# Five tiles in the sweeps over the weight units, sign rows made in one go at the start, attention's operands loaded ahead of the weights, and a new search of the order

## The chip, the cores and the metric

The kernel runs on one core of one Trainium2 chip. A core has five engines, each with its own instruction queue worked off strictly in order: TensorE (PE, matrix products), VectorE (DVE), ScalarE (ACT), GpSimd (POOL) and SyncE (SP, which here issues every DMA). They wait for each other through semaphores. The metric is the device time of one execution in microseconds (us), lower is better; several executions are timed and the median is given.

## The reference

Two parts follow each other. The first is a chunked linear attention with decay (4 batches, 8 heads, 768 positions, head size 32, state size 16); the second multiplies its output with two weight matrices, with `h - tanh(h)` between them.

```python
cum = np.cumsum(la, axis=-1)                      # la = log(clip(a))
L = np.exp(cum[:, :, :, None] - cum[:, :, None, :]) * causal
M = np.einsum('bhin,bhjn->bhij', Cc, Bc) * L
y = np.einsum('bhij,bhjd->bhid', M, xc) + np.einsum('bhin,bhnd->bhid', Cc, state) * decay_to_i
state = decay_full * state + np.sum(Bx, axis=2)
...
x = attn_out.transpose(0, 2, 1, 3).reshape(3072, 256)
h = x @ w_in                                      # 3072 x 256 by 256 x 2048
out = (h - np.tanh(h)) @ w_out                    # 3072 x 2048 by 2048 x 256
```

`w_in` and `w_out` arrive as 64-bit floats, and the kernel makes 32-bit pairs of them itself.

## The kernel before, in words

**Second part.** The 3072 rows are 12 tiles of 256. The 2048 inner columns are 8 *units* of 256. One step (t, u) takes tile t through unit u: `mm1` (L646, twelve matmuls into `ph`), tanh on ACT (L661), the difference on DVE (L665), a rounded copy `gh` on ACT (L669) and the rest `gl` on DVE (L676), and `mm2` (L709, twelve matmuls into `o`). Each 32-bit operand is a rounded part plus a rest (`wh`, `wl`; `xh`, `xl`; `gh`, `gl`), and three of the four products are taken. Two steps named in `FULL`, (0, 0) and (0, 1), come before those parts are ready: they use the whole 32-bit operands (L630, L701). `conv(u)` turns unit u's raw 64-bit weights into `wh` and `wl`: two ACT passes (L348, L369) and five DVE passes (L353, L358, L361, L365, L372). `NSW` says how many tiles go through the weights in *sweeps* while those are still being converted: the first `NSW` tiles go through units 0 and 1, then all of them through 2 and 3, and so on (`SWEEPS`), with partial sums kept in `pt` tiles (L724, L731). The other tiles run through all eight units in one go.

**First part.** A batch's 768 positions are 7 chunks of up to 112, so there are 28 chunks. Chunks 0 to 2 belong to tile 0, 3 and 4 to tile 1, 5 and 6 to tile 2, and so on. For a chunk, PE makes the score products and the differences of `cum` into `att` (L512, L521), ACT takes the exponential (L536), DVE multiplies (L540), POOL clears the upper half (L543), and PE makes the output and the next state in `y` (L569, L575). ACT then copies the state into the next chunk's operand (four copies, L580) and the output into `xh` (L593), and DVE makes `xl` (L598); the next chunk's `y` needs those state copies. From chunk `joint` on, the products of the next chunk are issued together with this chunk's `y`. The three chunks of tile 0 use an older path (`first_tile`): PE makes `cp` from the logs `la` (L447, four matmuls for a half chunk), ACT takes the exponential with the bias `ncum` (L465), and DVE multiplies with `att` (L458 on PE, L470 on DVE). From chunk 3 on, the differences come from one matmul over 9 rows of `lt_c` and `rt_c`. Those rows are parts of `cum` (DVE makes `parts`, L875 to L879; a DMA puts them in DRAM, L882; eight DMAs for each of two spans of chunks bring them back, L888 and L890) beside rows of ones (`lt_c`, POOL memset, L827) and rows of signs (`rt_c`, L496: `lt_c`'s ones times a per-partition 0 or -1 `par`; four instructions, two for chunks 3 to 9 and two for chunks 10 to 27).

**The start.** `a` is loaded, clipped on DVE (L804) and its log taken on ACT (L840, `la`). PE makes the running sums `pr` and `pq` (L863, L868). Meanwhile PE runs `warm`, matmuls of ones that nothing reads (L834).

**What sets the order.** Every operation is registered with an engine and an assumed cost. A list scheduler walks through them with a priority per operation from the table `RANK`, and each engine's program is issued in the order of the starts that come out. Where the plan leaves PE idle for more than `SPARE` within its first 65 us, `fill` puts matmuls of ones there (L434), so many pieces as the gap holds, with `LATE` more for gaps over 2 us. They stand in PE's queue like any other instruction, and PE has to work them off before it goes on.

Of the kernel before, what the change touches and what calls it, by code (L numbers as in the profile page):

```python
# [15 lines left out]
ALU = mybir.AluOpType  # L16
# [26 lines left out]
NPH, NL, NSW, NRAW, NGB, LAG, WARM = 2, 3, 4, 2, 3, 2, 8  # L43
SWEEPS = 0, 2, 4, 6, 8
AHEAD = 32
LULL, SPARE, PIECE, LATE = 65.0, 0.35, 0.215, 1.4
NPT = 6
# [955 lines left out]
```

## Time and profile before

| | us |
|---|---|
| median of 3 runs | 336.06 |
| lowest and highest of them | 334.4, 338.8 |
| profiled execution: its own time | 337.54 |
| its span from first to last instruction | 335.8 |

Of the profile, busy shares of the engines say how much of the span an engine had an instruction running. A matmul of ones counts as busy too, and so does a matmul at half clock. So for PE the list of instructions in order of time has to be read beside the shares: it shows what is work and what is filler. In these lists a row begins with the start and the duration in us; the number behind "x" counts instructions, and the bracket at its end gives the idle time ahead and what ended it. A 32-bit matmul appears as two records, so a row of the program's order with x3 is x6 in the trace.

### The profile page before, as it was taken

How to read it: one execution, taken by the hardware profiler on the slowest of the kernel's cores; microseconds unless marked ns; L12 is line 12 of the kernel's file. 1: busy time of each engine (PE TensorE's matmuls, PEld its weight loads, DVE VectorE, ACT ScalarE, POOL GpSimd, SP SyncE). 2: the span in 40 equal slices, each digit the busy share in tenths (PEclk: the TensorE clock that was granted, in tenths of full speed). 3: DMA queues.
4: the chain of work that ended last, by engine and by line, in shares of the span. 5: the costliest groups of instructions: out<-in, count | busy, mean ns of one | idle time of the engine just before them, and what ended most of it. 6: DMA issues, size and time to landing. Idle time of an engine off the chain costs nothing.

```text
span 335.8 us, 9087 instructions
## 1 busy us (share of the span) xinstructions
PE 326.6 (97%) x3872; PEld 314.4 (94%) x3872; DVE 226.6 (67%) x332; ACT 192.0 (57%) x404; POOL 56.8 (17%) x74
## 2 busy tenths in 40 slices
PE   8899999999999999999999999999999999999995
PEld 6788789999999999999999999999999999999995
DVE  2779999999998975645555655655655655654552
ACT  5766888784775644344555645643656645644441
POOL 6543464610102110000011101101111101100000
PEclk9699999999999999999999999999999999999999
DMA  6939668640102102010011200200200100100000
GB/s 158 263 112 307 153 230 193 194 143 0 48 9 68 32 0 65 31 33 2 31 48 31 64 12 20 64 20 13 62 4 2 33 2 2 33 0 2 31 2 32
DMA packets 12472, 21.41 MB, mean 64 GB/s; under 512 B 2848, under 2 KB 7648, under 8 KB 12432
## 3 DMA queue, kind: packets, MB, share of 16 engines
q1 hardware_dynamic: 12432, 20.84, 21.9%
q8 instruction: 30, 0.49, 0.6%
q14 instruction: 10, 0.08, 0.1%
HBM read 17.51 MB, written 3.32 MB: 62 GB/s over the span
## 4 chain that ended last, share of the span: by engine, by line
PE 87%; DMA 4%; DVE 4%; issue 2%; ACT 1%; POOL 1%; SPq 1%; POOLq 0%
PE o L709 39%; PE ph L646 38%; PE y L569 4%; PE att L521 3%; DMA bc<-bc_d 3%; DMA raw<-w_d 2%; PE att L512 1%; PE cp L447 1%; PE y L575 1%; POOL lt L543 1%; DVE lt L470 1%; DVE wm L353 0%; DVE g L665 0%; PE att L458 0%; DVE rt_c L496 0%
## 5 line engine op out<-in xcount | busy, mean ns | idle before, releaser
L665 DVE TENSOR_TENSOR g<-ph,g 128x512 f32<-128x512 f32 x96 | 66.1, 690 | 55.9 <-ACT g L661 55.9
L661 ACT ACTIVATE g<-ph 128x512 f32<-128x512 f32 x96 | 57.5, 599 | 74.3 <-PE ph L646 71.7
L646 PE MATMUL ph<-xh,wh 128*128 128x256 f32 x376 | 95.3, 278 | 0.2 <-DVE g L665 0.2
L646 PE MATMUL ph<-xh,wl 128*128 128x256 f32 x376 | 94.5, 276 | 0.0
L676 DVE TENSOR_TENSOR gl<-g,gh 128x512 fp32r<-128x512 f32 x94 | 66.7, 713 | 26.6 <-ACT gh L669 24.0
L669 ACT CAST gh<-g 128x512 fp32r<-128x512 f32 x94 | 58.2, 619 | 36.0 <-DVE g L665 29.7
L646 PE MATMUL ph<-xl,wh 128*128 128x256 f32 x376 | 73.2, 276 | 0.0
L646 PEld LDWEIGHTS ph<-xh,wh 128*128 128x128 f32 x376 | 70.6, 188 | 0.8 <-DVE g L665 0.4
L646 PEld LDWEIGHTS ph<-xh,wl 128*128 128x128 f32 x376 | 70.6, 188 | 0.0
L709 PE MATMUL o<-gh,wh 128*128 128x256 f32 x376 | 60.2, 282 | 0.0
L709 PE MATMUL o<-gh,wl 128*128 128x256 f32 x376 | 57.9, 276 | 0.0
L709 PE MATMUL o<-gl,wh 128*128 128x256 f32 x376 | 57.9, 276 | 0.0
L646 PEld LDWEIGHTS ph<-xl,wh 128*128 128x128 f32 x376 | 56.6, 188 | 0.0
L709 PEld LDWEIGHTS o<-gh,wh 128*128 128x128 f32 x376 | 49.8, 188 | 1.1
L709 PEld LDWEIGHTS o<-gh,wl 128*128 128x128 f32 x376 | 49.6, 188 | 0.0
L709 PEld LDWEIGHTS o<-gl,wh 128*128 128x128 f32 x376 | 49.6, 188 | 0.0
L543 POOL TENSOR_SCALAR_AFFINE_SELECT lt<-lt 128x896 f32<-128x896 f32 (+1 forms) x25 | 28.6, 1143 | 122.3 <-DVE lt L540 109.5
L540 DVE TENSOR_TENSOR lt<-att,lt 128x896 f32<-128x896 f32 (+1 forms) x25 | 26.6, 1065 | 2.8 <-ACT lt L536 2.1
L396 POOL TENSOR_TENSOR bw<-braw,wdec 128x256 f32<-128x256 f32 x14 | 12.3, 886 | 90.7 <-PE y L575 89.9
L536 ACT ACTIVATE lt<-att 128x896 f32<-128x896 f32 (+1 forms) x25 | 22.6, 904 | 1.4 <-PE att L521 0.3
L580 ACT COPY x<-y 16x64 f32<-16x64 f32 x96 | 19.4, 202 | 6.4 <-DVE xl L598 3.5
L569 PE MATMUL y<-lt,x 128*32 128x112 f32 (+1 forms) x448 | 16.8, 268 | 1.9 <-POOL lt L543 1.2
(79 smaller groups left out, 264.1 us busy)
## 6 DMA issues: line engine op xcount, KB each, us to landing
raw<-w_d SPq DMA_DIRECT2D x16, 512.0 KB
x<-x_d SPq DMA_DIRECT2D x14, 256.0 KB
bc<-bc_d SPq DMA_DIRECT2D x56, 60.0 KB
out_d<-ob SPq DMA_DIRECT2D x16, 128.0 KB
braw<-bn_d SPq DMA_DIRECT2D x14, 112.0 KB
out_d<-pt SPq DMA_DIRECT2D x8, 128.0 KB
cum<-parts SPq DMA_DIRECT2D x1, 168.0 KB
lt_c<-cum SPq DMA_DIRECT2D x4, 27.0 KB
```

What stands on the lines that cost most here:

```text
L396: nc.gpsimd.tensor_tensor(out=d["b"].rearrange("p c (h n) -> p c h n", h=H), in0=d["braw"].rearrange("p c (h n) -> p c h n", h=H), in1=wd. ...
L536: nc.scalar.activation(k["l"][:, :, 0:q].rearrange("p (i w) q -> p i w q", i=4), place[1][:, :, 0:2, N : N + q], AF.Exp)
L540: nc.vector.tensor_tensor(out=lt, in0=place[1][:, :, 2:4, N : N + q], in1=lt, op=ALU.mult)
L543: nc.gpsimd.affine_select(out=k["l"][:, :, 0:q], in_=k["l"][:, :, 0:q], pattern=[[0, H], [1, q]], compare_op=ALU.is_ge, fill=0.0, base=N, ...
L569: nc.tensor.matmul(out=y[D * h : D * h + D, hg * Q : hg * Q + q], lhsT=d["x"][:, cg, P * hg + D * h : P * hg + D * h + D], rhs=k["l"][:, 4 ...
L580: nc.scalar.copy(grp[(ck + 1) // CPG]["x"][0:N, (ck + 1) % CPG, 2 * D * i : 2 * D * i + 2 * D], k["y"][D * i : D * i + N, H * D : H * D + ...
L646: nc.tensor.matmul(out=ph[:, j, :], lhsT=w_[:, u, 0, k, j * P : (j + 1) * P], rhs=d[("xh", "xl")[p]][:, k, ts], start=p == 0 and k == 0 an ...
L661: nc.scalar.activation(g, gs[t, u][0], AF.Tanh)
L665: nc.vector.tensor_tensor(out=g, in0=ph, in1=g, op=ALU.subtract)
L669: nc.scalar.copy(gh, gs[t, u][1])
L676: on.tensor_tensor(out=gl, in0=g, in1=gh.bitcast(F32), op=ALU.subtract)
L709: nc.tensor.matmul(out=po[t, seg][:, e, :], lhsT=w_[:, u, 1, j, e * P : (e + 1) * P], rhs=g[:, j, :], start=u == seg[0] and k == 0 and j = ...
```

## The change

- `NSW` goes from 4 to 5: tiles 0 to 4 go through the weights in sweeps. `joint` moves with it from chunk 10 to chunk 12, and three more sums into `pt` and one more copy take the place of the fifth tile's last copies. `NPT`, the number of `pt` buffers, goes from 6 to 7, and a smaller reserve (`dynamic_dma_scratch_size`) makes room for it.
- The four instructions that make the sign rows (L496, each behind `lt_c`'s ones) go. In their place DVE sets all of `rt_c` from chunk 3 on to 1 at the start, and multiplies it twice with `par`, the second time in place.
- `warm` grows from 8 to 10 matmuls.
- `LATE` shrinks from 1.4 to 0.6, and the planner's assumed lag behind a DMA grows, most for POOL.
- `RANK` is a new table, so nearly every instruction of the first 70 us stands elsewhere.

```diff
-NPH, NL, NSW, NRAW, NGB, LAG, WARM = 2, 3, 4, 2, 3, 2, 8
+NPH, NL, NSW, NRAW, NGB, LAG, WARM = 2, 3, 5, 2, 3, 2, 10
-LULL, SPARE, PIECE, LATE = 65.0, 0.35, 0.215, 1.4
-NPT = 6
+LULL, SPARE, PIECE, LATE = 65.0, 0.35, 0.215, 0.6
+NPT = 7
 RANK = """
-147 351 639 203 244 86 296 353 131 427 266 928 811 84 242 227 476 72 88 71 191 74 773 287 117 117 324 209 273 250 172
+21 1082 131 136 347 155 106 120 1250 704 221 751 237 279 665 53 610 117 277 109 215 33 80 335 59 1220 245 342 212 803
...
     def lag(self, a, b):
-        return self.DMA_LATENCY if a == "DMA" else 0.0 if a == b else self.SEM_PE if "PE" in (a, b) else self.SEM
+        if a == "DMA":
+            return {"POOL": 2.4, "DVE": 1.3, "ACT": 1.3}.get(b, self.DMA_LATENCY)
+        return 0.0 if a == b else self.SEM_PE if "PE" in (a, b) else self.SEM
...
-                for w in range(2):
-                    op("DVE", (0.45, 0.8)[s], lambda w=w, sl=sl: nc.vector.tensor_scalar(
-                           out=rt_c[:, w, sl], in0=lt_c[:, sl], scalar1=par[:, w : w + 1], scalar2=None, op0=ALU.mult),
-                       r=[l_c[s], "par", k["n_l"][1]], w=[r_c[s]])
...
+    sign = [rt_c[:, w, SPAN[0].start :].rearrange("p c m -> p (c m)") for w in range(2)]
+    op("DVE", 0.9, lambda: nc.vector.memset(sign[0], 1.0), w=r_c)
+    for w in (1, 0):
+        op("DVE", 0.95, lambda w=w: nc.vector.tensor_scalar(out=sign[w], in0=sign[0], scalar1=par[:, w : w + 1], scalar2=None,
+                                                            op0=ALU.mult), r=["par"], w=r_c)
...
-    nc = bacc.Bacc("TRN2", target_bir_lowering=False, num_devices=1)
+    nc = bacc.Bacc("TRN2", target_bir_lowering=False, num_devices=1, dynamic_dma_scratch_size=1024)
```

Three places of the new order matter below. The first is DVE's queue at its very start. Before, the clip of `a` (L804) stands right behind two small memsets:

```order
L790 MEMSET a_sb 32x32
L804 TENSOR_SCALAR a_sb<-a_sb 128x224
L807 TENSOR_SCALAR pid<-pid 128x1
L808 TENSOR_SCALAR pid<-pid 128x1
L809 CAST pidf<-pid 128x2
L810 CAST ncf<-ncol 128x16
L811 TENSOR_SCALAR par<-pidf 128x1
L812 TENSOR_SCALAR par<-pidf 128x1
L813 TENSOR_SCALAR idn<-ncf,pidf 128x16
L353 TENSOR_SCALAR wm_163<-raw_126 128x512
```

Now the same place of DVE's queue reads as follows (`rt_c` are the sign rows, 3200 numbers of two bytes on each partition):

```order
L790 MEMSET a_sb 32x32
L847 MEMSET rt_c 128x3200
L807 TENSOR_SCALAR pid<-pid 128x1
L808 TENSOR_SCALAR pid<-pid 128x1
L809 CAST pidf<-pid 128x2
L810 CAST ncf<-ncol 128x16
L811 TENSOR_SCALAR par<-pidf 128x1
L812 TENSOR_SCALAR par<-pidf 128x1
L813 TENSOR_SCALAR idn<-ncf,pidf 128x16
L849 TENSOR_SCALAR rt_c<-rt_c,par 128x3200 x2
L804 TENSOR_SCALAR a_sb<-a_sb 128x224
L882 CAST parts<-rows 112x2x128
```

The clip of `a`, from which the logs and all of attention follow, moved behind the constants and the three new instructions.

The second place is PE's queue from chunk 0's `y` to chunk 2's `y`. Before, with `pq` as the target of the filler:

```order
L569 MATMUL y_268<-lt_186,x_141 32x112 x8
L575 MATMUL y_268<-x_141,bw_212 16x32 x8
L458 MATMUL att<-bc_161 128x112 x8
L447 MATMUL cp_1_302<-upto,la 128x112 x4
L434 MATMUL pq_178<-const-float32-1.0 32x128 x3
L569 MATMUL y_331<-lt_234,x_141 32x112 x8
L575 MATMUL y_331<-x_141,bw_212 16x32 x8
L434 MATMUL pq_178<-const-float32-1.0 32x128 x22
L569 MATMUL y_403<-lt_287,x_144 32x112 x8
```

And now:

```order
L569 MATMUL y_266<-lt_196,x_133 32x112 x8
L575 MATMUL y_266<-x_133,bw_181 16x32 x8
L462 MATMUL att<-bc_156 128x112 x8
L451 MATMUL cp_1_305<-upto,la 128x112 x4
L438 MATMUL pq_165<-const-float32-1.0 32x128 x2
L569 MATMUL y_333<-lt_237,x_133 32x112 x8
L575 MATMUL y_333<-x_133,bw_181 16x32 x8
L438 MATMUL pq_165<-const-float32-1.0 32x128 x17
L569 MATMUL y_400<-lt_286,x_291 32x112 x8
```

The work is the same; six pieces of filler fewer stand in it. Behind it, three groups of filler of 5, 2 and 2 pieces become one of 11, which stands between chunk 6's `y` and the products of chunk 8.

The third place is SP's queue of DMAs at the start. Before:

```order
L315 DMA braw_99<-bn_d 112x256
L792 DMA a_sb<-a_d 112x192
L794 DMA a_sb<-a_d 96x32
L325 DMA raw_126<-w_d 128x1024
L294 DMA bc_128<-bc_d 16x960 x4
L325 DMA raw_126<-w_d 128x1024
L306 DMA x_141<-x_d 128x512
L306 DMA x_144<-x_d 128x512
```

And now:

```order
L792 DMA a_sb<-a_d 112x192
L319 DMA braw_99<-bn_d 112x256
L794 DMA a_sb<-a_d 96x32
L310 DMA x_133<-x_d 128x512
L298 DMA bc_143<-bc_d 16x960 x4
L329 DMA raw_150<-w_d 128x1024
L329 DMA raw_150<-w_d 128x1024
L298 DMA bc_156<-bc_d 16x960
```

Unit 0's weights (`raw`) moved behind the first chunk's operands `x` and `bc`. Further down, the second half of unit 1's weights is now the fifth DMA behind the one that puts `cum`'s parts into DRAM (L887 now, L882 before); it was the fourth, and the first half stood behind it too, which now stands ahead.

96 rows, old and new, of the table RANK are left out of this document.

## The prediction

> **What bounds the kernel now.** I read the page first: busy time, then the slices. Columns of the first row: engine, busy us, share, instructions; then the busy share of PE and its granted clock in 40 slices, in tenths.
>
> ```profile
> PE 326.6 (97%) x3872; PEld 314.4 (94%) x3872; DVE 226.6 (67%) x332; ACT 192.0 (57%) x404; POOL 56.8 (17%) x74
> ...
> PE   8899999999999999999999999999999999999995
> ...
> PEclk9699999999999999999999999999999999999999
> ```
>
> PE is the bound, and behind the first five slices (8.4 us each) it is never short of work. So a change of order can win only what PE wastes early: idle time, filler, and work at half clock. The list of PE's instructions in order of time shows it (start, duration, what; in the bracket the idle time ahead):
>
> ```profile
> 0.84 3.59 PE L834 MATMUL warm<-const-float32-1.0 128*32 128x128 f32 x16 [0.84 <-PEq L993]
> 4.66 0.66 PE L863 MATMUL pr<-upto,la 128*112 128x128 f32 x4 [0.23 <-POOL after L799]
> ...
> 6.81 1.04 PE L447 MATMUL cp<-upto,la 128*128 128x112 f32 x8
> 9.55 0.71 PE L458 MATMUL att<-bc 16*128 16x112 f32 x16 [1.70 <-POOL bc L403]
> 10.19 1.14 PE L447 MATMUL cp<-upto,la 128*128 128x112 f32 x8
> 11.71 1.21 PE L458 MATMUL att<-bc 16*128 16x112 f32 x16 [0.38 <-DVE lt L470]
> 12.85 3.75 PE L447 MATMUL cp<-upto,la 128*128 128x112 f32 x16
> 16.54 0.98 PE L569 MATMUL y<-lt,x 128*32 128x112 f32 x16
> ...
> 19.56 0.85 PE L434 MATMUL pq<-const-float32-1.0 128*32 128x128 f32 x6
> 21.05 0.59 PE L569 MATMUL y<-lt,x 128*32 128x112 f32 x16 [0.64 <-ACT x L580]
> ...
> 21.66 4.83 PE L434 MATMUL pq<-const-float32-1.0 128*32 128x128 f32 x42
> 26.28 0.30 PE L569 MATMUL y<-lt,x 128*32 128x112 f32 x3
> ...
> 32.58 0.59 PE L569 MATMUL y<-lt,x 128*32 128x112 f32 x16 [0.52 <-POOL lt L543]
> ...
> 38.25 1.28 PE L434 MATMUL ph<-const-float32-1.0 128*32 128x128 f32 x10
> ...
> 40.17 0.63 PE L434 MATMUL ph<-const-float32-1.0 128*32 128x128 f32 x4
> 41.50 0.59 PE L569 MATMUL y<-lt,x 128*32 128x112 f32 x16 [0.70 <-POOL lt L543]
> ...
> 46.45 0.61 PE L434 MATMUL ph<-const-float32-1.0 128*32 128x128 f32 x4
> ```
>
> The reader is to see two things. Four `cp` matmuls take 1.04 us at 6.81, but eight take 3.69 from 12.85 to 16.54, 1.85 for four, or 1.77 times as much. The windows show why (PEclk is the granted clock):
>
> ```profile
> 11.00:12.00 1.00, 0.62 (x7) 0.45 (x10) 0.66 (x2) 1.00 (x4) 0.89 (x2) 0.63 1.00 122
> 12.00:13.00 1.00, 1.00 (x17) 0.80 (x15) 0.00 (x0) 0.68 (x3) 0.31 (x1) 0.50 1.14 186
> ...
> 18.00:19.00 1.00, 1.00 (x20) 0.89 (x17) 0.30 (x1) 0.67 (x4) 0.00 (x0) 0.95 0.56 160
> ```
>
> The clock is 0.63 in the twelfth microsecond and 0.95 in the nineteenth, so half from about 11.3 to 18.1, 6.8 us, after the idle 1.70 and 0.38. Second, I can split the opening at 26.28, where chunk 2's `y` begins. Behind it PE wastes 1.28 + 0.63 + 0.61 = 2.5 us on filler and 0.52 + 0.70 = 1.2 idle: 3.7 in all. Ahead of it stands everything else, and that part hangs on when `la` is ready.
>
> **The change, part by part.** (a) The start. DVE, then ACT, in order of time:
>
> ```profile
> 0.91 0.24 DVE L789 MEMSET a_sb<- 16x224 f32 x1 [0.91 <-PEq L993]
> 1.20 0.09 DVE L790 MEMSET a_sb<- 32x32 f32 x1
> 3.60 0.28 DVE L804 TENSOR_SCALAR a_sb<-a_sb 128x224 f32<-128x224 f32 x1 [2.31 <-DMA a_sb<-a_d]
> 3.94 0.15 DVE L807 TENSOR_SCALAR pid<-pid 128x1 int32<-128x1 int32 x1
> ...
> 4.64 0.33 DVE L813 TENSOR_SCALAR idn<-ncf,pidf 128x16 f32<-128x16 f32 x1
> ```
>
> ```profile
> 3.90 0.61 ACT L840 ACTIVATE la<-a_sb 128x224 f32<-128x224 f32 x1 [1.61 <-DVE a_sb L804]
> ...
> 5.83 0.20 ACT L817 ACTIVATE tab<-const-float32-1.0 128x1 f32<-128x1 f32 x1
> 7.60 0.68 ACT L348 ACTIVATE wv<-raw 128x512 f32<-128x512 f32 x1 [1.57 <-DMA raw<-w_d]
> 8.18 0.35 ACT L873 COPY rows<-pr 112x256 f32<-112x256 f32 x1
> ```
>
> Before, `a`'s DMA ends the wait of L804, and DVE has been idle for 2.31 us. Now the memset of 3200 numbers, the constants (3.94 to 4.97, 1.0 us) and two multiplications stand ahead. No row shows these sizes. From the groups of equal shape:
>
> ```profile
> L496 DVE TENSOR_SCALAR rt_c<-lt_c,par 128x2304 bf16<-128x2304 bf16 x2 | 2.1, 1066 | 0.0
> ...
> L496 DVE TENSOR_SCALAR rt_c<-lt_c,par 128x896 bf16<-128x896 bf16 x2 | 1.1, 608 | 0.0
> ```
>
> The memset: by L789's whole row 0.24 / 224 x 3200 = 3.4 us, by the difference of L789 and L790 (0.15 us for 192 numbers) 2.5; the lower end is as quick as L496, 1066 + 896 x (1066 - 608) / 1408 = 1.64 us. I take 3.1, between the two readings of DVE's own memset and nearer to the one that counts a whole instruction. The two multiplications are then 2 x 1.64 = 3.3 by the same line; but L496's back-to-back starts lie 0.1 us closer than its durations, and the 1066 is a mean of two rows, so I take 2.6, with 2.2 and 3.3 as ends. L804 starts at 1.29 + 3.1 + 1.0 + 2.6 = 8.0 instead of 3.60, 4.4 us later.
>
> [...]
>
> Most of the delay has cover. Before, ACT reached `rows` and `ncum` only from 8.18 on, since it waited 1.57 us for weights ahead of it in its queue. Now no weights stand there: `la` 8.3, PE's first sum 0.76 behind `la`'s start (4.66 - 3.90), at 9.1. But PE has then been idle since `warm`'s end (0.84 + 3.59 and four more records, about 4.9), 4.2 us, more than the 1.70 behind which the clock fell. So I take half clock here. The sums and eight `cp` of chunk 0 take 4.66 to 7.85, 3.2 us, at full clock, 5.6 at half: PE ends them at 14.7 (12.3 at full clock). Half clock lasted 6.8 us before; from 8 (an idle stretch behind 4.9) that reaches to 14.8, so I price what follows at full clock. POOL's copy into `bc`, on which chunk 0's `att` waits, stood ahead of the product `bw` in POOL's queue and stands behind it now:
>
> ```profile
> 8.99 0.51 POOL L403 COPY bc<-idn 128x64 f32<-128x64 f32 x1 [2.89 <-DMA bc<-bc_d]
> 10.30 1.33 POOL L396 TENSOR_TENSOR bw<-braw,wdec 128x256 f32<-128x256 f32 x1 [0.80 <-ACT wdec L904]
> ```
>
> `bw` needs `wdec`, which ACT now makes first behind `tab`, 2.1 us behind `la`'s start (5.83 + 0.20 - 3.90), from 10.4 to 10.8. With 1.33 and 0.51 the copy ends at 12.7: hidden at half clock, and the later one at full clock.
>
> (b) From there to chunk 2's `y`. PE's list: `att` 0.65 three times (9.55 to 10.19), `cp` 1.05 four times, chunk 0's `y` 0.65, 2 pieces of filler 0.46 (a piece is two records of 4.83 / 42 = 0.115), chunk 1's `y` 0.65, 17 pieces 3.9: 11.8 us. Chunk 1's `y` waits 0.7 more, as now (0.64), since DVE's `xl` of chunk 0 stands behind a product of chunk 1 in DVE's queue. So chunk 2's `y` starts at 14.7 + 12.5 = 27.2, against 26.28: **+0.9**. Fewer filler pieces (22 to 17, 1.15 us) and the shorter cold stretch here pay for most of the later start.
>
> (c) Behind it. Filler 11 x 0.23 = 2.5, as now. The idle 1.2 waited for POOL's L543, behind DVE. The four sign instructions (3.3 us by their groups) leave DVE there, so PE's waits should shrink; ends 0 and 1.2, I take 0.6: **-0.6**.
>
> (d) `joint`. Two chunks more have their products apart from `y`. From the chain (start, us, what):
>
> ```profile
> 168.78 1.57 PE o L709 x12
> 170.35 1.36 PE ph L646 x12
> ```
>
> A step behind 32-bit work takes 1.57 instead of 1.36, so two more such changes cost 2 x 0.21 = **+0.4**; ends 0 and 0.4.
>
> (e) Five tiles in the sweeps, `NPT`, the copies: no time in PE's list, since PE is full there already and does the same twelve matmuls; their cover is PE's own work. With five tiles each unit's conversion (five DVE passes) lies beside a quarter more PE work, but no wait for it is left to win. `warm`'s two matmuls lie in the wait for `la`. SP's new start: weights of unit 0 are used by ACT behind two `lt`, at 15 or later, so later landing is covered. The scratch size and the planner's lag issue nothing.
>
> Sum: 0.9 - 0.6 + 0.4 = +0.7 on the profiled 337.54. The median of the runs is 336.06, 1.5 lower; on it I forecast **336.8 us**, no change that a measurement of this kernel could tell (about 2%, 6.7 us).
>
> [...]
>
> **The rivals.**
>
> *The opening stays warm or gets short.* If the memset runs as quickly as L496, 1.64 instead of 3.1, and PE is not throttled, its sums end at 12.3 - 1.5 = 10.8; POOL's copy, also 1.5 earlier at 11.2, is the later. Then chunk 2's `y` starts at 11.2 + 12.5 = 23.7, and the sum is -2.6 - 0.6 + 0.4 = -2.8: 333.3. For it: DVE has a quick form for two-byte numbers, as L496 shows; against: L789. Chance 0.25.
>
> *Slower: the half clock lasts.* Its place is the work between 14.7 and 27.2, 11.8 us of PE instructions, at 1.77 times. Six more microseconds of half clock hold 3.4 us of that work, 2.6 us lost: 339.4. It passes 2% (342.8) only if about 7.8 us of that work, nearly 14 us of time, stay at half, until about 28.5. For it: before, the clock stayed at half from 12 to 18 while PE was busy throughout. Chance 0.15, of which 0.04 beyond 2%.
>
> *Weights of unit 1 come late.* Their second half stands behind the parts of `cum` in SP's queue, whose wait ended at 10.21 and now ends near 13 (`rows` follows `wdec` and `ncum`, 2.7 later than 8.18). It was issued thus:
>
> ```profile
> 10.21 0.33 SPq L882 DMA_DIRECT2D cum<-parts  x1
> ...
> 13.96 0.42 SPq L325 DMA_DIRECT2D raw<-w_d  x1
> ```
>
> So it goes out at about 16, and landing 5.4 us later (the first weights, issued at 2.18, were used at 7.60) it is there at 21.5; the conversion reaches it near 24. If that slack of 2.5 us is gone, each us costs one, as ACT's state copies stand behind the conversion: at 2 us, 338.8. Chance 0.1.
>
> **How the numbers follow.** My forecast 0.5, the others as above. Ends of the terms: memset 1.64 to 3.4, multiplications 2.2 to 3.3, idle behind 26.28 0 to 1.2, clock 12.3 or 14.7 or later. The quick case with no idle gives 332.7, the lasting clock with the slow ends 340.8; 332 to 340.5 leaves out less than 2 in 10. Faster by over 2% (below 329.3) needs another 3 us beyond the quick case: 0.05. Slower by over 2%: 0.05. Within: 0.9.
>
> **What would show it.** Right: L804 near 8, the memset near 3 us, the clock at half when the sums run, chunk 2's `y` near 27, one filler of 22 records behind it, no wait on PE after 65 us. Wrong: a memset near 1.6; full clock at 9 to 15, or half beyond 18; ACT waiting for `raw` ahead of the state copies; waits of PE on DVE or DMAs within the sweeps, which I take as none.

## The result and the profile after

The changed kernel took 340.57 us (median of 7 runs, 339.77 to 343.48); the kernel before took 336.28 beside it (7 runs). The ratio is 1.0138, with a 95% interval of 1.0096 to 1.0179: slower by 1.4%, less than the 2% that such a comparison is judged by, but clearly outside its own scatter. The profiled execution took 340.36 us, with a span of 338.6 against 335.8 before. Runs more than 1.5% above the fastest of the same kernel (405.94 us at a granted clock of 0.753 in run 5, 537.36 at 0.56 in run 6, and a few less far off) are left out of the ratios and of the counts of runs.

The page of the profile looks almost as before: PE is busy for about the same time (325.6 us against 326.6), and only the first slices differ.

```profile
PE 325.6 (96%) x3868; PEld 313.9 (93%) x3868; DVE 227.2 (67%) x333; ACT 191.5 (57%) x404; POOL 55.1 (16%) x74
...
PE   4979999999999999999999999999999999999995
...
PEclk9699999999999999999999999999999999999999
```

The first slice of 8.4 us shows PE busy for 0.4 of it, where it was 0.8. DVE's list in order of time says what happened there (start, duration, what, and in the bracket the idle time ahead):

```profile
1.20 0.09 DVE L790 MEMSET a_sb<- 32x32 f32 x1
2.01 2.73 DVE L847 MEMSET rt_c<- 128x3200 bf16 x1 [0.73 <-issue]
4.65 0.10 DVE L807 TENSOR_SCALAR pid<-pid 128x1 int32<-128x1 int32 x1
...
5.32 2.68 DVE L849 TENSOR_SCALAR rt_c<-rt_c,par 128x3200 bf16<-128x3200 bf16 x2
7.91 0.46 DVE L804 TENSOR_SCALAR a_sb<-a_sb 128x224 f32<-128x224 f32 x1
```

The clip of `a` (L804) starts at 7.91 instead of 3.60. PE's list shows what that becomes:

```profile
0.84 3.65 PE L834 MATMUL warm<-const-float32-1.0 128*32 128x128 f32 x20 [0.84 <-PEq L998]
9.16 1.08 PE L873 MATMUL pq<-la,after 128*128 128x224 f32 x2 [4.67 <-ACT la L840]
...
11.64 2.94 PE L451 MATMUL cp<-upto,la 128*128 128x112 f32 x16
14.52 0.71 PE L462 MATMUL att<-bc 16*128 16x112 f32 x16
...
19.25 0.30 PE L575 MATMUL y<-x,bw 128*16 128x32 f32 x16
21.18 0.71 PE L462 MATMUL att<-bc 16*128 16x112 f32 x16 [1.63 <-issue]
...
23.89 0.59 PE L569 MATMUL y<-lt,x 128*32 128x112 f32 x16 [0.36 <-POOL lt L479]
...
28.43 0.59 PE L569 MATMUL y<-lt,x 128*32 128x112 f32 x16
...
34.82 0.59 PE L569 MATMUL y<-lt,x 128*32 128x112 f32 x16 [0.71 <-POOL lt L543]
...
46.52 2.61 PE L438 MATMUL ph<-const-float32-1.0 128*32 128x128 f32 x22
```

Three things are to be seen. PE waits 4.67 us for `la`. Chunk 2's products (the `att` at 21.18) wait 1.63 us, which before they did not. And chunk 2's `y` starts at 28.43 instead of 26.28, 2.15 us later, while the span is longer by 2.8. So three quarters of the loss lie ahead of this point, where the prediction had put its cut, and 0.65 us behind it.

### The profile page after: what moved, and what is told of

It reads as the page before. It is cut to its first block, busy times and chain, and to the rows that moved or that the text cites. A ratio compares the mean times of both kernels' runs of the same rounds, so it can differ in the third digit from the quotient of the medians.

```text
span 338.6 us, 9085 instructions
## 1 busy us (share of the span) xinstructions
PE 325.6 (96%) x3868; PEld 313.9 (93%) x3868; DVE 227.2 (67%) x333; ACT 191.5 (57%) x404; POOL 55.1 (16%) x74
## 4 chain that ended last, share of the span: by engine, by line
PE 85%; DVE 6%; issue 5%; POOL 1%; ACT 1%; DMA 1%; SPq 0%; POOLq 0%; DVEq 0%
PE o L709 38%; PE ph L646 36%; PE y L569 3%; PE att L521 2%; PE cp L451 2%; PE att L512 1%; DVE rt_c L847 1%; DVE lt L540 1%; PE y L575 1%; DMA bc<-bc_d 1%; PE att L462 1%; POOL lt L543 1%; POOL lt L479 1%; PE o L701 1%; DVE gl L676 1%
## 5 line engine op out<-in xcount | busy, mean ns | idle before, releaser
L676 DVE TENSOR_TENSOR gl<-g,gh 128x512 fp32r<-128x512 f32 x94 | 64.7, 690 | 24.5 <-ACT gh L669 22.6
L543 POOL TENSOR_SCALAR_AFFINE_SELECT lt<-lt 128x896 f32<-128x896 f32 (+1 forms) x25 | 28.4, 1136 | 122.8 <-DVE lt L540 109.9
L400 POOL TENSOR_TENSOR bw<-braw,wdec 128x256 f32<-128x256 f32 x14 | 10.5, 751 | 103.5 <-PE y L575 101.8
```

Of the source, the lines that this page charges most:

```text
L400: nc.gpsimd.tensor_tensor(out=d["b"].rearrange("p c (h n) -> p c h n", h=H), in0=d["braw"].rearrange("p c (h n) -> p c h n", h=H), in1=wd. ...
L543: nc.gpsimd.affine_select(out=k["l"][:, :, 0:q], in_=k["l"][:, :, 0:q], pattern=[[0, H], [1, q]], compare_op=ALU.is_ge, fill=0.0, base=N, ...
L676: on.tensor_tensor(out=gl, in0=g, in1=gh.bitcast(F32), op=ALU.subtract)
```

## The experiments

All were compared with the kernel before on their own chip. Behind chunk 2's `y` little separates them, as this table shows: its last column, the span less the start of chunk 2's `y`, lies between 309.3 and 310.7 us in all profiles. What decides is when that `y` starts, which varies by 5.6 us.

| kernel | PE's first sum | chunk 2's `y` | span of the profile | median, us | ratio (95%) | behind `y` |
|---|---|---|---|---|---|---|
| before, first profile | 4.66 | 26.28 | 335.8 | 336.28 | | 309.5 |
| before, second profile | 4.64 | 23.17 | 332.5 | 334.62 | 0.9989 (0.9956 to 1.0022) | 309.3 |
| after, first profile | 9.16 | 28.43 | 338.6 | 340.57 | 1.0138 (1.0096 to 1.0179) | 310.2 |
| after, second profile | 9.16 | 28.19 | 338.4 | 340.09 | 1.0144 (1.0109 to 1.0180) | 310.2 |
| 1 before, sign rows ahead of the clip | 8.65 | 27.10 | 337.2 | 339.04 | 1.0121 (1.0089 to 1.0152) | 310.1 |
| 2 after, clip ahead of the sign rows | 5.08 | 25.51 | 335.9 | 337.51 | 1.0067 (1.0039 to 1.0094) | 310.4 |
| 3 after, chunk 1's product earlier | 9.16 | 27.46 | 337.7 | 339.60 | 1.0132 (1.0101 to 1.0164) | 310.2 |
| 4 after, `warm` with 18 more | 9.16 | 26.20 | 336.4 | 338.83 | 1.0127 (1.0086 to 1.0168) | 310.2 |
| 6 after, sign rows made as before | 5.22 | 25.63 | 335.7 | 337.27 | 1.0034 (1.0005 to 1.0062) | 310.1 |
| 7 after, short ones, then the clip | 5.22 | 24.45 | 334.9 | 336.34 | 1.0028 (0.9996 to 1.0059) | 310.5 |
| 8 as 7, chunk 1's product earlier | 5.22 | 22.82 | 333.3 | 337.21 | 1.0050 (1.0012 to 1.0087) | 310.5 |
| 9 as 6, chunk 1's product earlier | 5.19 | 23.95 | 334.6 | 336.32 | 1.0029 (1.0000 to 1.0058) | 310.7 |
| 10 before, short sign rows at the start | 4.69 | 22.85 | 333.0 | 335.56 | 1.0001 (0.9961 to 1.0040) | 310.2 |

Runs 5 and 11 are the second profiles of before and after.

**1. The sign rows alone, in the kernel before.** Theory 1 was that the sign rows ahead of the clip, with PE at half clock behind them, are nearly the whole loss.

```diff
-                    op("DVE", (0.45, 0.8)[s], lambda w=w, sl=sl: nc.vector.tensor_scalar(
-                           out=rt_c[:, w, sl], in0=lt_c[:, sl], scalar1=par[:, w : w + 1], scalar2=None, op0=ALU.mult),
+                    op("DVE", (0.45, 0.8)[s], lambda: None,
...
+    def signs():
+        nc.vector.memset(sign[0], 1.0)
...
+            nc.vector.tensor_scalar(out=sign[w], in0=sign[0], scalar1=par[:, w : w + 1], scalar2=None, op0=ALU.mult)
-    op("DVE", 0.28, logs, r=["al"], w=["a"])
+    op("DVE", 0.28, lambda: (signs(), logs()), r=["al"], w=["a"])
```

> The kernel before with one part of the change alone: its four late sign instructions go, and the memset, the constants and the two multiplications stand ahead of the clip of a on DVE. Theory 1 (the start: the clip of a stands behind the sign rows, and PE's clock falls in the longer idle stretch): the clip starts near 8 instead of 3.6 us, chunk 2's y between 28 and 30 instead of 26.3, the time 339 to 341 against 336.3. Theory 2 (the new order and the five tiles cost it, the start is covered): the time stays at 336 or falls, since DVE is relieved of 3 us where it is busiest.

Measured: 339.04 us, ratio 1.0121. The changed kernel itself stands at 1.0138 and 1.0144. So this one edit, with the old table, four tiles in the sweeps and the old weights' place, gives some 85% of the loss by the middles of the intervals. Chunk 2's `y`, at 27.10, came earlier than the 28 to 30 expected. PE's list of this run, in order of time:

```profile
8.65 1.17 PE L870 MATMUL pr<-upto,la 128*112 128x128 f32 x4 [4.22 <-ACT la L847]
...
10.36 1.89 PE L447 MATMUL cp<-upto,la 128*128 128x112 f32 x8
...
12.80 1.04 PE L447 MATMUL cp<-upto,la 128*128 128x112 f32 x8
```

Behind 4.22 us of idle time four `cp` take 1.89 us, and 2.4 us later the same four take 1.04. So PE was at half clock here, and then at full clock. The clock record that is kept with this trace has its first entry, of full clock, at 12.78 us: nothing in it says that PE was at full clock at any time before.

**2. The clip first, in the changed kernel.** The memset and the two multiplications go behind the clip, while the constants stay ahead of it; everything else stays.

In the code one line moves the recorded operations in the planner's order, the clip (`logs`) ahead of the ones and the signs, all behind `a`'s loads (`al`, `a2`) and POOL's constants:

```diff
+    op.moves = [([m["consts"], m["logs"], m["ones"], m["sign", 1], m["sign", 0]], [m["al"], m["a2"], m["pool"]])]
```

> The changed kernel, with the constants and the clip of a moved ahead of the three sign instructions on DVE, all else in its place. Theory 1: the clip starts at 3.6 us, but the sign rows then hold the parts of cum on DVE until about 9.3; chunk 2's y at 24.5 to 25.5 instead of 28.4, the time 336.5 to 337.5 against 340.6. Theory 2: within 1 us of 340.6.

Measured: 337.51 us, ratio 1.0067. About half of the loss is gone, though PE's first sums run 4.1 us earlier. PE now lost time further back:

```profile
8.86 0.71 PE L467 MATMUL att<-bc 16*128 16x112 f32 x16 [0.58 <-POOL bc L412]
...
12.17 1.21 PE L467 MATMUL att<-bc 16*128 16x112 f32 x16 [1.52 <-DVE lt L479]
13.31 3.76 PE L456 MATMUL cp<-upto,la 128*128 128x112 f32 x16
```

Chunk 1's `att` waits for DVE, which was busy with the sign rows until 9.80 and then with `parts` until 11.24, and behind that wait PE is at half clock (3.76 us for eight `cp`).

**3. The missed wait.** In the changed kernel the list says "issue" for the 1.63 us ahead of chunk 2's products: the trace names no releaser. The first three chunks share one `att` tile, and the rows suggest that a chunk's products start when DVE has done its first multiplication (L474) with those of the chunk before. For chunk 2 that is the one at 20.47, which ends at 21.09, just ahead of 21.18 (in runs 6 and 7 the same two moments are 16.09 and 16.19, 16.54 and 16.64), and in DVE's list it stands behind five instructions of the weight conversion:

```profile
17.09 0.62 DVE L474 TENSOR_TENSOR lt<-att,lt 128x448 f32<-128x448 f32 x1 [1.09 <-PE att L462]
17.63 0.42 DVE L357 TENSOR_SCALAR wm<-raw 128x512 uint32<-128x512 uint32 x1
...
20.13 0.42 DVE L362 TENSOR_SCALAR wv<-wv 128x512 f32<-128x512 f32 x1
20.47 0.62 DVE L474 TENSOR_TENSOR lt<-att,lt 128x448 f32<-128x448 f32 x1
```

The experiment puts chunk 1's first product directly behind chunk 0's second one:

```diff
+    op.moves = [([m["m", 1, 0]], [m["m", 0, 1], m["x", 1, 0]])]
```

> The changed kernel, with chunk 1's first product on DVE moved ahead of five conversion instructions of unit 0's weights, all else in its place. Theory 1: PE's idle 1.63 us ahead of the products of chunk 2 goes, chunk 2's y comes 1 to 1.5 us earlier, the time is 339.2 to 339.8: the smaller part of the loss. Theory 2 (this wait is the loss): 337 to 338.

Measured: the wait is gone, as PE's list shows, and 1.00 us of another has come in:

```profile
19.35 0.30 PE L580 MATMUL y<-x,bw 128*16 128x32 f32 x16
19.58 0.71 PE L467 MATMUL att<-bc 16*128 16x112 f32 x16
...
22.92 0.59 PE L574 MATMUL y<-lt,x 128*32 128x112 f32 x16 [1.00 <-POOL lt L484]
...
27.46 0.59 PE L574 MATMUL y<-lt,x 128*32 128x112 f32 x16
```

Chunk 2's `y` is 0.97 us earlier than in the changed kernel. The time, 339.60 with ratio 1.0132 against 1.0138 and 1.0144, says no more than that the gain is small. That those conversion instructions were the cause of the wait is shown by its going; that the shared tile is what links the two is read from the rows alone.

**4. Keeping PE warm.** The changed kernel with 18 more `warm` matmuls in its wait for `la`.

```diff
-        for i in range(WARM):
+        for i in range(WARM + 18):
```

> The changed kernel with 18 more warm-up matmuls, so that PE has no idle stretch ahead of the sums. If the half clock between 7 and 13.6 us is a cost: the clock stays full, the eight cp of chunk 0 end at 12.3 instead of 14.5, the time falls by about 2, to 338.5. If ACT and POOL hold that stretch anyway: the time stays at 340.6 and products of chunk 0 start where they did, at 14.5.

Measured: 338.83 us, ratio 1.0127. Three of the six runs lie near 338.1, two near 341.0 and one at 339.5. The profile is of the first group:

```profile
10.43 1.93 PE L451 MATMUL cp<-upto,la 128*128 128x112 f32 x16
```

Eight `cp` take 1.93 us instead of 2.94, and chunk 2's `y` starts at 26.20 instead of 28.43. So half clock in the opening is worth 2.2 us in the profile. The ratios, 1.0127 against 1.0138 and 1.0144, do not tell the two kernels apart: the other three runs have granted clocks of 0.990 to 0.994, and where PE lost its clock in them no profile shows. The rest of the loss, the late start itself and the wait of 1.63 us ahead of chunk 2's products, is still in this profile.

**5. The kernel before once more.** By now the spans (+2.8) and the medians (+4.3) did not agree. The suspicion was that the profiled execution of before was a dear one.

> The kernel before, unchanged, for a second profile and for the granted clock of each of its runs. Theory 1 (the profiled execution that the prediction was worked on was one of its dearer ones: half clock from 11.3 to 18.1 made chunk 2's y start at 26.28, and most runs do not have it): most runs at a granted clock of 0.998 or more and 334.0 to 335.5 us, the others at 0.989 to 0.994 and 336.5 to 338; if the profile falls on a run at full clock, the eight cp matmuls behind 12 us take about 2 us and not 3.7, and chunk 2's y starts between 23 and 24.5. Rival (the two groups of times have nothing to do with the opening): in a run at 334 to 335 chunk 2's y still starts near 26.3 and the difference lies behind it.

Measured: 334.62 us. The second profile, of a run of 334.24 us, has this in PE's list:

```profile
9.07 0.71 PE L458 MATMUL att<-bc 16*128 16x112 f32 x16 [0.37 <-POOL bc L403]
...
11.88 2.04 PE L447 MATMUL cp<-upto,la 128*128 128x112 f32 x16
...
17.81 0.59 PE L569 MATMUL y<-lt,x 128*32 128x112 f32 x16 [0.75 <-ACT x L580]
...
23.17 0.58 PE L569 MATMUL y<-lt,x 128*32 128x112 f32 x16
```

The eight `cp` that took 3.75 us in the first profile take 2.04, POOL's `bc` made PE wait 0.37 and not 1.70, and chunk 2's `y` starts at 23.17, 3.1 us earlier. Both profiles are of the same program. The second is not free of half clock either: its first sum takes 1.17 us and not 0.66, and the clock record begins with full clock at 6.43 us, where that of the first profile begins at 4.44. PE so came to the wait for `bc` 0.85 us later, and `bc` itself was ready 0.48 earlier, which makes the shorter wait. Of 94 runs of this kernel, timed in and beside the experiments 1 to 10, 65 have a mean granted clock of 0.997 or more and a median of 334.58 us; 17 lie at 0.990 to 0.994 with 336.14, and 10 at 0.983 to 0.989 with 338.03. The first profile, 0.989 and 337.54, belongs to the dearest.

**6. The rest of the change without its sign rows.** The changed kernel with the sign rows made by the four old instructions behind chunk 0's and chunk 2's products.

```diff
-    op("DVE", 0.9, lambda: nc.vector.memset(sign[0], 1.0), w=r_c)
+    op.mark["ones"] = op("DVE", 0.9, lambda: old_signs(0), w=r_c)
...
+    op.moves = [([m["ones"]], [m["m", 0, 1]]), ([m["sign", 1]], [m["m", 2, 1]])]
```

> The changed kernel with the sign rows made as before: no memset of 3200 and no two multiplications at the start, the four instructions behind chunk 0's and chunk 2's products instead; everything else (five tiles in the sweeps, the new order, attention's operands ahead of the weights) stays. Theory 1 (the early sign rows are the whole loss and the rest of the change is worth about nothing): the clip runs near 3.6, PE's first sums near 5, chunk 2's y starts between 22.5 and 24.5, and the time is 334 to 336. Rival A (the rest of the change costs something by itself): 337 or more with the clip early. Rival B (the rest is a gain that the sign rows hid): below 333.5.

Measured: 337.27 us, ratio 1.0034 (1.0005 to 1.0062). Rival A came true (337 or more with the clip early), not theory 1. PE's list and the windows (the sixth number behind the stretch's length is the granted clock) show the missed wait again, and what it brings:

```profile
16.19 1.01 PE L467 MATMUL att<-bc 16*128 16x112 f32 x16 [2.30 <-issue]
17.13 2.05 PE L456 MATMUL cp<-upto,la 128*128 128x112 f32 x8
```

```profile
16.00:17.00 1.00, 0.81 (x16) 0.77 (x16) 0.09 (x1) 0.00 (x0) 0.58 (x1) 0.73 1.03 201
...
23.00:24.00 1.00, 1.00 (x10) 0.92 (x9) 1.00 (x2) 0.00 (x0) 0.18 (x1) 0.85 1.03 381
```

Behind the wait of 2.30 us the clock is at half, from about 16.5 to 23.3. Two sign instructions (1.13 us) now stand in DVE's queue ahead of the five of the conversion, which makes the wait longer than the 1.63 of the changed kernel. So the new order has a loss of its own, which in the changed kernel stands beside the larger one.

**7 and 8. The sign rows in half the instructions' length.** Two ones of 16 bits make one word of 32, so the memset has 1600 elements instead of 3200. It stands ahead of the clip, in DVE's wait for `a`'s DMA, and the multiplications behind the clip. Run 8 adds the edit of run 3.

```diff
+TWO_ONES = struct.unpack("<f", struct.pack("<I", 0x3F803F80))[0]
...
-    op("DVE", 0.9, lambda: nc.vector.memset(sign[0], 1.0), w=r_c)
+    op.mark["ones"] = op("DVE", 0.9, lambda: nc.vector.memset(sign[0].bitcast(F32), TWO_ONES), w=r_c)
```

> The changed kernel with the ones of the sign rows written as 1600 words of 32 bits (two ones in each), that memset first on DVE, then the clip, then the constants and the two multiplications. Theory 1 (the memset's time goes by elements, and what counts is when the clip and the parts of cum are ready): the memset takes 1.3 to 1.5 us and ends before a's DMA lets the clip start at 3.6, so it is hidden; parts come near 8.5 where the clip ahead of a memset of 2.7 gave 9.71; chunk 2's y starts between 22.5 and 24.5 and the time is 334 to 335.5. Rival A (the time goes by bytes): the memset stays at 2.7 us, the clip comes at about 4, time 336 to 337. Rival B (half clock decides and comes all the same): chunk 2's y at 25 or later, 336.5 to 337.5.

> The same with chunk 1's first product ahead of the conversion instructions in DVE's queue (the edit that took 1.6 us of idle time from PE, and 1 us from chunk 2's y). Theory 1: chunk 2's y 0.5 to 1 us earlier than without this edit, time 333 to 335, at or a little below the kernel before. Rival (the filler in front of chunk 2's y and the waits behind it are fixed, so an earlier product only moves the wait): the same time as without the edit, within 0.3 us.

Measured: DVE's list of run 7, at its start, reads

```profile
1.68 1.39 DVE L853 MEMSET rt_c<- 128x1600 f32 x1 [0.40 <-issue]
3.92 0.32 DVE L810 TENSOR_SCALAR a_sb<-a_sb 128x224 f32<-128x224 f32 x1 [0.85 <-DMA a_sb<-a_d]
```

The memset takes half as long and is hidden: the clip waits for the DMA again. Run 7 took 336.34 us, where theory 1 had 334 to 335.5, and its profile still has the wait of 1.63 us ahead of chunk 2's products and half clock behind it. Run 8 has no such wait and, in its profile (335.0 us), full clock from 6.51 us on and chunk 2's `y` at 22.82. That is as early as in the second profile of before, but more than half of its runs took 337 us or more, at granted clocks of 0.98 to 0.993, and the median is 337.21. Theory 1's time was met in the profile and missed in the median.

**9. Both losses undone.** Run 6 with the edit of run 3.

> The changed kernel with the sign rows made as before and, besides, chunk 1's first product ahead of the conversion instructions in DVE's queue: both losses found so far undone, all else of the change kept. With the sign rows alone undone, chunk 2's products waited 2.30 us, the clock fell to a half behind that wait, chunk 2's y started at 25.63 and the time was 337.3. Theory 1 (the two losses are the sign rows ahead of the clip and that one wait, and each brings half clock with it; the rest of the change gains some 1 to 1.5 us in the opening and loses some 0.7 behind chunk 2's y): no wait of PE over 1 us ahead of chunk 2's y, full clock there in most runs, chunk 2's y between 21.3 and 22.3, and a time of 333 to 334.5, a little below the kernel before or equal to it. Rival (the wait only moves to chunk 1's y, since DVE has as much to do as before, and the clock falls there): y of chunk 1 waits 1.5 us or more, chunk 2's y at 24 or later, 336 or more.

Measured: 336.32 us, ratio 1.0029 (1.0000 to 1.0058). The rival's way came true: the wait moves on, as PE's list shows, and behind it the clock falls after all.

```profile
17.62 0.59 PE L574 MATMUL y<-lt,x 128*32 128x112 f32 x16 [1.70 <-POOL lt L484]
...
23.95 0.59 PE L574 MATMUL y<-lt,x 128*32 128x112 f32 x16 [1.88 <-ACT x L585]
...
25.38 5.23 PE L635 MATMUL ph<-whole,wv 128*128 128x256 f32 x16
```

Until 25 us the granted clock reads full. In the next four microseconds it reads 0.52, 0.50, 0.50 and 0.77, half for 3.4 us, and the first products of the second part (L635) take 5.23 us where the other profiles have 3.72. These 1.5 us lie behind chunk 2's `y`, and the last column of the table is largest for this run.

`ACT x` (L585) waits ahead of chunk 2's `y` for DVE's `xl`, which stands behind the two sign instructions of the second span (1.86 us) and the conversion. From 9 to 24 us DVE is the busiest engine, 13.72 of 15 us, with PE at 11.20:

```profile
9.00:24.00 15.00, 11.20 (x174) 10.02 (x174) 13.72 (x24) 10.10 (x36) 7.46 (x10) 1.00 0.79 203
```

**10. Short sign rows in the kernel before.** The old order and table, the four sign instructions gone, the short memset ahead of the clip and the multiplications behind the constants.

```diff
-    op("DVE", 0.28, logs, r=["al"], w=["a"])
+    op("DVE", 0.28, lambda: (sign_ones(), logs()), r=["al"], w=["a"])
...
-    op("DVE", 0.9, consts_dve, r=["pid"], w=["idn", "par"])
+    op("DVE", 0.9, signs, r=["pid"], w=["idn", "par"])
```

> The kernel before, in its own order, with the four sign instructions behind the first chunks' products gone and the sign rows made at the start so that nothing waits for them: the ones as 1600 words of 32 bits first on DVE, inside its wait for a's DMA, then the clip and the constants as before, then the two multiplications of 3200 in DVE's wait for the first weights. Theory 1 (the early sign rows cost only by standing ahead of the clip; DVE is the engine that sets chunk 2's y, and 1.9 us of sign work less between 13 and 22 us brings it forward): the clip near 3.6 to 3.9, PE's first sums near 5, y of chunk 1 without its 0.75 of idle time, chunk 2's y at 22 to 22.8 instead of 23.17 in a run at full clock, and 333.3 to 334.2 us there, 0.5 to 1 us below the kernel before. Rival A (the multiplications of 2.7 us still delay what follows them on DVE, the parts of cum and the conversion, and slow POOL's copies beside them, as POOL's three copies took 3.1 instead of 1.1 us in the runs that had them side by side): att of chunk 0 waits for POOL's bc by 0.7 us or more, chunk 2's y at 23 or later, 334.5 to 335.5. Rival B (the added idle time brings half clock in most runs): 336.5 or more.

Measured: 335.56 us, ratio 1.0001 (0.9961 to 1.0040). Run 1 differs from it in the memset's length and in what stands ahead of the clip, and this is the cleanest pair of the study: 1.0121 and 1.0001. Early sign rows cost nothing that this measurement can tell (0.4% at most) if the clip does not wait for them. They also gain nothing that can be measured, against theory 1: 42 records of filler (4.83 us) stand in PE's queue ahead of chunk 2's `y`, so DVE's earlier end moves it only from 23.17 to 22.85.

**11. The changed kernel once more,** on another chip.

> The changed kernel unchanged, on the chip of the other experiments, for a second profile and for the granted clock of its runs. Theory 1 (the late first sums make PE idle 4.2 to 4.7 us in every run, which is always enough to halve the clock, where the kernel before idles for 1.7 us at most and is halved in about a third of its runs only): no run at a granted clock of 0.997 or more, a median of 340 to 341, a ratio of 1.013 to 1.019, chunk 2's y between 27.5 and 28.5 and the wait of 1.6 us ahead of chunk 2's products. Rival (the half clock of its first profile was chance, as that of the kernel before was): some runs at full clock and 338, chunk 2's y near 26.2 in them.

Measured: 340.09 us, ratio 1.0144, the wait of 1.64 us and chunk 2's `y` at 28.19, as theory 1 had it. Its "no run at a granted clock of 0.997 or more" fails: four of six runs show a granted clock of 0.999. But they took 339.94 to 340.12 us, little less than the two at 0.990 (340.64 and 340.85), and the profile of one has eight `cp` in 2.71 us where full clock takes 1.93 (run 4):

```profile
0.84 4.44 PE L834 MATMUL warm<-const-float32-1.0 128*32 128x128 f32 x20 [0.84 <-PEq L998]
...
11.64 2.71 PE L451 MATMUL cp<-upto,la 128*128 128x112 f32 x16
```

The clock record of this profile has its first entry, of full clock, at 13.25 us. In the first profile of the changed kernel PE reached full clock at 3.51, during `warm` (3.65 us there, 4.44 here), and lost it again at 6.92. So PE ran the first sums at half clock in both: in one the record shows the fall in the wait for `la`, in the other it shows no full clock ahead of 13.25; and no run was quick.

## Why the prediction was wrong

The prediction was 336.8 us, range 332.0 to 340.5, and no change that could be told. The time came out at 340.57, just above the range.

*Part (a), the start, held.* L804 was forecast at 8.0 and started at 7.91; PE's first sum at 9.1 and came at 9.16; the eight `cp` were to end at 14.7 and `att` followed at 14.52. The clock was forecast at half from 8 to 14.8; the windows show 0.96 in the seventh microsecond, 0.50 in the next six and 0.62 from 13 to 14, so half from about 6.9 to 13.8. That PE reaches full clock and loses it in the wait is what this profile shows; in run 11 the record has no full clock ahead of 13.25, when those sums are over. L804's start was right in part by luck, as two errors cancel: the memset took 0.26 more than forecast, the constants 0.33 less (0.67, from 4.65 to 5.32), and the multiplications were right (2.59 for 2.6). One sum was wrong: by the line through L496's two sizes, 3200 numbers take 1066 + 291 ns = 1.36 us and not 1.64, which makes two multiplications 2.7 and the quick memset of the first rival 0.3 quicker still.

The memset was put at 3.1 us. Its row reads 2.73, but from the end of the row ahead (1.29) to the start of the next one (4.65) are 3.36 us, if the 0.73 that the trace calls "issue" is counted with it (runs 1 and 2 have 3.37 and 3.38 in the same way). Of the prediction's two readings of DVE's own memset, L789's whole row (3.4) was the one that came closest to this. In run 7, 1600 elements of four bytes took 1.39 us, 0.87 ns each; here 3200 of two bytes took 2.73, 0.85 ns each.

*Part (b) failed.* It priced the way from the end of `cp` to chunk 2's `y` at 12.5 us, 11.8 of work and 0.7 of waiting; it took 28.43 - 14.52 = 13.9, with 1.63 + 0.36 = 2.0 us of waiting. The work, 11.9, was right. The wait was wrong: the prediction carried over the 0.7 from before and put no price on what stands ahead of chunk 1's first multiplication in DVE's new queue. Run 3, and run 9 beside run 6, show that it is those five conversion instructions. That is 1.3 us. Since the eight `cp` ended 0.2 earlier than forecast, +0.9 became +2.15.

*Part (c) failed as well.* The idle time behind chunk 2's `y` was to shrink from 1.2 to 0.6 when the sign instructions leave DVE. The waits of PE, summed by releaser (total, times, longest), say otherwise:

```profile
PE pq L873 <- ACT la L840: 4.7, 1, 4.7
PE att L462 <- issue: 1.6, 1, 1.6
PE y L569 <- POOL lt L543: 1.0, 2, 0.7
PE warm L834 <- PEq L998: 0.8, 1, 0.8
PE att L512 <- DVE lt L540: 0.4, 1, 0.4
PE y L569 <- POOL lt L479: 0.4, 1, 0.4
```

Behind 28.43 stand the 1.0 and the 0.4 on DVE, 1.4 in all. In the first profile of before it was 0.52 + 0.70 and another 0.23 at 68.70, which the prediction left out: 1.45. The filler is 2.61 against 2.5. So this part gave +0.1 instead of -0.6: one wait on POOL's L543 went (0.70), and two others came, at 58.99 and 61.66 (0.29 and 0.39). *Part (d)*, +0.4 for `joint`, can't be told apart. Behind chunk 2's `y` the changed kernel has 0.65 us more than the first profile of before, but run 1 and run 10, with the old order there, have 0.6 and 0.7 more as well. What this time is stays open.

*The basis failed, and this is the largest single piece.* The sum, +0.7, was made on an execution that already paid for half clock, and 1.5 us was then taken off to reach the median, as if the same share of half clock stood in both. Before, half clock ahead of chunk 2's `y` is chance: run 5 shows that most runs are without it or with little, at 334.6. After, both profiles have it over the first sums, and none of the 13 runs lies below 339.77. By the sum the forecast was 1.25 short in (b) and 0.85 in (c) and (d); the step to the medians makes up for the other 1.7: the median after is 0.2 above its profile, and that of before 1.3 below its own.

*The rivals.* The quick opening did not come: the memset took 3.36 and not 1.64. L849's multiplications took 0.40 ns for each of the same 3200 two-byte numbers (2.59 us for both), the memset's row 0.85. The lasting half clock did not come: it ended at 13.8. Weights of unit 1 were not late: ACT reaches them at 25.76 and DVE at 26.08, both without waiting for a DMA. Two rivals were missing from the list: a multiplication of chunk 1 behind the conversion in DVE's queue, and a profile of before that was dear by chance. Of what was announced as signs of being wrong, one showed, and small: PE waits 0.39 us for DVE at 61.66 (before, 0.23 at 68.70). All but 0.65 us of the loss lay ahead of 29 us.

## What to carry to other kernels

An instruction without inputs that is put early is free only where its engine waits for something, so put the memset into the wait for the first DMA and the rest behind the operation that the longest chain starts from: the sign rows cost 1.2% ahead of the clip, and nothing measurable with a memset half as long in the wait and the multiplications behind the clip. When an order is made anew, read each engine's queue for what stands ahead of the instructions that others wait for, since a wait that goes at one place (runs 3 and 9) comes back where that engine is the busiest. And before a sum is made on one profiled execution, compare that execution with the lowest of the runs: if it holds a chance price, the change may make that price certain.

## What the runs showed of the hardware

**Half clock in the opening lasted 3.4 or 6.8 us in these profiles.** Worked out from the shares at both ends of the windows, it lasted from 11.3 to 18.1 in the first profile of before, 11.6 to 18.4 in run 2, 16.5 to 23.3 in run 6, 6.9 to 13.8 in the changed kernel (6.8 us each), 25.0 to 28.5 in run 9 and, as here, 17.0 to 20.5 in run 7 (3.4 us each):

```profile
17.00:18.00 1.00, 1.00 (x17) 0.80 (x11) 0.34 (x1) 0.00 (x0) 0.25 (x1) 0.52 0.65 197
...
20.00:21.00 1.00, 1.00 (x37) 0.95 (x36) 0.72 (x2) 1.00 (x4) 1.00 (x2) 0.77 0.11 29
```

The stretches at full clock between the first entry of the record and the fall were 3.41 us in the changed kernel, 6.83 in run 2 and in the first profile of before, 10.24 in runs 6 and 7, 20.48 in run 9. The clock was at half behind 1.63 us of idle time in run 7, 1.52 in run 2 and 1.88 in run 9, and was not behind 1.63 in the changed kernel or 1.70 in run 9; what makes the difference stays open. Nor does a row say why the first full clock of one program, the kernel before, came at 4.44 us in one profile and at 6.43 in the other.

**The record of the clock can begin late, and its first entry is of full clock.** That entry stands at 4.44 us in the first profile of before and at 3.51 in that of the changed kernel. In runs 1 and 11 the granted clock reads 1.00 throughout the start, while `cp` runs at half speed (in run 1, 1.89 us for four, and 1.04 at 12.80): the record has no entry ahead of 12.78 and 13.25 us, and the views print 1.00 where it has none. Run 5 is alike until 6.43, runs 6, 7, 8 and 10 until 6.2 to 6.8. So a mean granted clock of 1.00 (run 1) or 0.999 (run 11) does not exclude half clock at the start. The durations of like matmuls are the surer sign.

**POOL's three copies into `braw` took 3.11 us beside DVE's two-byte multiplications, 1.07 without them.** The rows are from run 5 and run 8 (POOL's lists). In run 5 DVE had nothing to do from 4.95 to 7.12; in run 8 DVE's two multiplications of 3200 ran beside them, from 4.86 to 7.54, and the copies ended 0.6 us behind those:

```profile
5.02 1.07 POOL L822 COPY braw<-idn 16x256 f32<-16x256 f32 x3
```

```profile
5.01 3.11 POOL L828 COPY braw<-idn 16x256 f32<-16x256 f32 x3 [0.90 <-DVE idn L819]
...
9.50 0.42 POOL L413 COPY bc<-idn 128x64 f32<-128x64 f32 x1
```

In the changed kernel, with the multiplications beside them from 5.32 to 8.00, they took 3.15, and in run 6, without, 1.11. In run 8 `bc`, which stands behind them in POOL's queue, was ready at 9.92 (7.69 in run 6), and PE waited 0.90 us for it. What slows the copies no row shows.
